# A hand-ordered attention and mixing kernel: order of work, PSUM banks and filling products laid anew

## Chip, core and metric

The kernel runs on one core of one Trainium2 chip. The metric is the device time of one execution in microseconds. The engines are TensorE (PE, matrix products; PEld is its weight load), VectorE (DVE), ScalarE (ACT), GpSimd (POOL) and SyncE (SP, here the one queue that issues all DMAs).

## What is computed

Eight batches of eight heads, 576 positions, head size 64. Attention with a mask over blocks of 64 positions comes first; its output, put together over the heads, goes through a mixing layer.

```
scores = scale * q @ k.T ; masked where block_i < block_j ; softmax over the last axis
x      = (attn @ v), heads side by side: (8, 576, 512)
theta  = x @ w_theta ; zr = x * cos(theta) ; zi = x * sin(theta)
y      = w_tok_r @ zr + w_tok_i @ zi        (over positions)
u      = x + y
out    = u + max(u @ w_ch, 0)
```

## The kernel before

**Tiling.** Two heads are one pair; there are 32 pairs (`p`), 64 heads (`n`), four pairs to a batch (`b`). The work is cut into 2757 named parts, each a few instructions, each with the parts that it needs, the PSUM banks that it takes and those that it leaves.

**A pair.** `q`, `k`, `v` load. `qh`, `ql`, `kh`, `kl` split q and k in two summands (from pair 12 on; before that the products are plain fp32). `sab`, `sc`, `sd` are the scores in three pieces (L596, L608): `sab` takes two banks for each head, `sc` one for each, `sd` one for both. `m` are negated row maxima (DVE, L634 or L626), `e` the exponentials (ACT, L638), which read the banks and leave them.

**A head.** `high` and `low` split the probabilities in two fp16 summands (`low` always on DVE, L665), `turn` transposes each by DMA (L669, SP queue). The first four pairs have `tp` and `cp` in their place: transposes on PE (L650) and copies out of PSUM (L657, L659). `weighted` are the products with V (L684), 42 or 45 small ones of 65 columns. All heads put them into bank 0, so head n+1 has to wait until `normalise` of head n has read it: add (L694 on DVE or L692 on ACT), reciprocal (L696), product (L701), and for odd heads a last piece (L704). `again` copies 64 rows (POOL, L710).

**V's scale.** For each batch `vz` sums |v| on ACT (L501), `vr` adds the two sums (DVE, L505), `vb` and `vm` spread the sum (L349, L355), `vc` makes a power of two of it (L362 to L371), and `vf` scales V (POOL, L576). Of the first batch all this stands ahead of head 0.

**A batch's mixing.** `theta` are the products for the angles (L784), five tiles, each in one bank; `turns` (ACT), `rest` (DVE, L800), `size` and `sines` (ACT, L818, L820) make cosine and sine; `z`, `zh`, `zl` (L830, L324 to L330, L843) multiply by x and split; `mix` are the products over positions (L853), in eight sums of five parts; `u` takes them (L866); `uh`, `ul` split; `c` are the channel products (L886), `out` adds (L892), `fin` scales, `store` writes. The mixing of a batch runs between the pairs of the next.

**The order is written out.** `order_of` sorts the parts by the numbers in `PLACES`, one for each part, and checks that each comes after what it needs. Every engine gets its own parts in this order and runs them strictly so; so does SP's queue. `BANKS` lists the PSUM bank for each taking part in that order. `RUNNING` lists filling products (L1107): `(11, 1, 3)` means that ahead of part 11 of the order three products of 512 columns go to bank 1, whose result nobody reads. Which engine does a part is told by `ON`, which the change doesn't touch.

Of the kernel before, what the change touches and what calls it, by code (L numbers as in the profile page):

```python
# [187 lines left out]


RUNNING = [  # L190
    (11, 1, 3), (15, 5, 4), (35, 0, 15), (43, 0, 1)
]
ON = {"w5": "DDADADADD",
      "wc": "DPDPPPDDP",
# [966 lines left out]
```

## Time and profile before

| | |
|---|---|
| median of the runs | 663.96 us (663.5, 663.96, 668.18) |
| the profiled execution | 662.92 us |
| its span, first to last instruction | 661.1 us |
| PE busy | 639.8 us, 7136 products |
| DVE, ACT, POOL busy | 568.9, 474.7, 319.9 us |
| filling products | 23 |

The profile is of one execution. An engine's busy time is the time in which at least one of its instructions ran; products on PE overlap, and their ends are modelled, so a short loss can hide in "busy". Idle time ahead of an instruction is shown with what ended it.

### The profile page before, as it was taken

To read this page: it belongs to the slowest core of one execution; us is meant where nothing else is said; L and a number is where in the kernel's file an instruction comes from. 1 tells how busy PE (TensorE), PEld (TensorE's weight loads), DVE (VectorE), ACT (ScalarE), POOL (GpSimd) and SP (SyncE) were. 2 spreads that over 40 slices of the span, in tenths; PEclk is the share of its full clock that TensorE was granted. 3 is DMA by queue.
4 is the path that set the end of the run, shared out by engine and by line. 5 is a ranking of instruction groups with operands and counts; after the bars stand their busy time and mean duration, and the time that the engine had idled before them with its cause. 6 is when DMAs were issued, how large, how long until landed. Compare 5 with 4: busy or idle time off the path is not lost.

```text
span 661.1 us, 17330 instructions
## 1 busy us (share of the span) xinstructions
PE 639.8 (97%) x7136; PEld 502.5 (76%) x7136; DVE 568.9 (86%) x891; ACT 474.7 (72%) x732; POOL 319.9 (48%) x341
## 2 busy tenths in 40 slices
PE   7999989999989999999999999999999999999997
PEld 4789757887678868787788768887778768785775
DVE  5899998999999999899988998999877989857624
ACT  4898797966998779666985679896976777525502
POOL 1422156642567437963455456447566354233900
PEclk9999989999999999999999999999999999999999
DMA  8874177999999998899946996999659986550002
GB/s 324 294 252 157 42 148 154 206 205 196 191 228 167 167 245 178 145 183 251 174 121 126 225 190 139 224 187 214 159 135 224 178 147 124 105 123 11 1 37 108
DMA packets 247647, 110.51 MB, mean 167 GB/s; under 512 B 229008, under 2 KB 229008, under 8 KB 247568
## 3 DMA queue, kind: packets, MB, share of 16 engines
q1 hardware_dynamic: 247568, 109.41, 75.7%
q8 instruction: 56, 0.92, 0.6%
q14 instruction: 23, 0.19, 0.1%
HBM read 43.06 MB, written 9.44 MB: 79 GB/s over the span
## 4 chain that ended last, share of the span: by engine, by line
PE 72%; DVE 12%; ACT 6%; DMA 5%; POOL 2%; issue 2%; SPq 0%; ACTq 0%; DVEq 0%; POOLq 0%
PE ps L853 28%; PE ps L784 12%; PE ps L886 11%; PE ps L684 11%; PE ps L596 9%; DVE m L634 4%; DMA w_raw<-in_w_tok 2%; DMA pt<-p 2%; DVE p L665 1%; ACT t L638 1%; DMA w_raw<-in_w_theta 1%; DVE wT_l L432 1%; PE ps L608 1%; ACT L638 1%; DMA q<-in_qT 1%
## 5 line engine op out<-in xcount | busy, mean ns | idle before, releaser
L638 ACT ACTIVATE t<-ps,m 128x320 f32<-128x320 f32 (+4 forms) x288 | 141.8, 554 | 46.7 <-DVE m L634 31.2
L853 PE MATMUL ps<-wT_h,zl 128*128 128x288 f16 x540 | 154.6, 286 | 1.5 <-POOL zl L843 1.5
L853 PE MATMUL ps<-wT_h,zh 128*128 128x288 f16 x540 | 154.9, 287 | 0.7 <-DVE sizes L362 0.7
L853 PE MATMUL ps<-wT_l,zh 128*128 128x288 f16 x540 | 154.5, 286 | 0.0
L634 DVE TENSOR_REDUCE m<-ps 128x2 f32<-128x640 f32 (+3 forms) x128 | 118.1, 945 | 16.3 <-PE ps L601 14.0
L853 PEld LDWEIGHTS <-zh 128*128 128x128 f16 x1080 | 105.9, 98 | 27.3 <-issue 0.9
L684 PE MATMUL ps<-v,pt 128*128 128x65 f16 (+2 forms) x2668 | 114.9, 202 | 7.3 <-DVE x_ring L701 2.2
L665 DVE SCALAR_TENSOR_TENSOR p<-t,p 128x1664 f16<-128x1664 f32 x56 | 110.1, 1967 | 0.4 <-ACT p L326 0.2
L886 PE MATMUL ps<-uhl,wch_h 128*128 128x288 f16 x512 | 95.3, 286 | 0.1
L684 PEld LDWEIGHTS <-pt 128*128 128x128 f16 x2436 | 82.3, 98 | 12.3 <-issue 6.3
L784 PE MATMUL ps<-wth_h,xt 128*128 128x512 f16 (+1 forms) x384 | 87.4, 345 | 0.0
L784 PEld LDWEIGHTS <-xt 128*128 128x128 f16 (+1 forms) x576 | 46.5, 102 | 43.3 <-issue 1.9
L326 ACT ACTIVATE p<-t 128x1664 f16<-128x1664 f32 x46 | 73.0, 1596 | 4.5 <-DMA pt<-p 3.8
L886 PE MATMUL ps<-uhl,wch_l 128*128 128x288 f16 x256 | 73.2, 286 | 0.0
L853 PEld LDWEIGHTS <-zl 128*128 128x128 f16 x540 | 52.9, 98 | 15.0 <-POOL zl L843 1.9
L886 PEld LDWEIGHTS <-wch_h 128*128 128x128 f16 x512 | 48.7, 98 | 13.3 <-issue 0.8
L784 PE MATMUL ps<-wth_l,xt 128*128 128x512 f16 (+1 forms) x192 | 57.3, 344 | 0.0
L710 POOL COPY x_ring<-x_ring 64x64 f32<-64x64 f32 x64 | 39.2, 613 | 36.7 <-DVE x_ring L701 21.2
L866 DVE SCALAR_TENSOR_TENSOR u<-ps,gain,u 128x288 f32<-128x288 f32 x64 | 31.5, 507 | 18.3 <-PE ps L853 18.0
L596 PE MATMUL ps<-kh,qh 64*128 64x288 f32 (+2 forms) x240 | 38.8, 312 | 2.9 <-ACT t L638 2.9
L596 PE MATMUL ps<-k,qh 64*128 64x224 f32 (+3 forms) x288 | 39.9, 407 | 1.5 <-DMA k<-in_kT 0.9
L794 ACT ACTIVATE aa<-ps,sizes 128x512 int32<-128x512 f32 (+1 forms) x40 | 25.2, 644 | 22.3 <-PE ps L784 22.1
(187 smaller groups left out, 1274.4 us busy)
## 6 DMA issues: line engine op xcount, KB each, us to landing
raw_v<-in_v SPq DMA_DIRECT2D x32, 384.0 KB, 4.5
q<-in_qT SPq DMA_DIRECT2D x32, 320.0 KB, 4.0
k<-in_kT SPq DMA_DIRECT2D x32, 320.0 KB, 3.9
out<-u SPq DMA_DIRECT2D x32, 288.0 KB, 3.9
w_raw<-in_w_tok SPq DMA_DIRECT2D x5, 576.0 KB, 5.4
p<-in_w_tok SPq DMA_DIRECT2D x4, 576.0 KB, 6.4
pt<-p SPq DMA_TRANSPOSE x112, 4.6
w_raw<-in_w_theta SPq DMA_DIRECT2D x2, 512.0 KB, 6.4
```

The source lines that it names most:

```text
L326: engine.mul(to, x, scale)
L596: nc.tensor.matmul(s[hh][:, col:col + n], lhsT=qq[rows, i * P:(i + 1) * P], rhs=kk[rows, k0:k0 + n], start=nn == 0 and (j == 0 or c == "ab ...
L634: nc.vector.tensor_reduce(out=m, in_=s, axis=AX.XY if i in (2, 3) else AX.X, op=ALU.max, negate=True)
L638: nc.scalar.activation(out=to, in_=s, func=AF.Exp, scale=1.0, bias=m)
L665: nc.vector.scalar_tensor_tensor(out=self.p[:, 1, :], in0=self.t, scalar=LIFT, in1=self.p[:, 0, :], op0=ALU.mult, op1=ALU.subtract)
L684: nc.tensor.matmul(to, lhsT=pp[:, block, :], rhs=x, start=nn == 0, stop=nn == n - 1)
L710: nc.gpsimd.tensor_copy(out=x[64 - 64 * hh:P - 64 * hh], in_=x[rows])
L784: nc.tensor.matmul(g[rows, 0:cols.stop - cols.start], lhsT=x[:, dt, part, i, rows], rhs=ww[:, dt, cols], start=(n == 0), stop=(n == 11))
L794: nc.scalar.mul(a[:, i, 0:n].bitcast(I32), bank("t", self.b, i)[:, 0:n], self.batch.turn)
L853: nc.tensor.matmul(g, lhsT=zz[:, kk, cols], rhs=ww[:, kk, ts], start=(n == 0 and kk == k0 and nn == 0), stop=(n == 4 and nn == 2))
L866: nc.vector.scalar_tensor_tensor(out=self.u(dt)[:, ts], in0=bank("y", self.b, dt, th)[:, 0:HS], scalar=g_y, in1=self.u(dt)[:, ts], op0=ALU ...
L886: nc.tensor.matmul(g[:, 0:HS], lhsT=ww[:, dt, e * P:(e + 1) * P], rhs=uu[:, dt, th * HS:(th + 1) * HS], start=(n == 0), stop=(n == 11))
```

## The change

Three lists are replaced: `PLACES` (2757 numbers), `BANKS` (361) and `RUNNING`. The functions, the parts, their needs, their engines and their instructions stay. The new order was laid starting from the executed one, with durations of its trace.

```diff
 PLACES = [
-    3, 2, 14, 22, 24, 61, 188, 190, 4, 5, 21, 30, 37, 65, 158, 178, 31, 28, 53, 60, 63, 106, 205, 259, 42, 45, 73,
...
+    3, 2, 16, 19, 21, 65, 162, 191, 4, 7, 25, 30, 32, 59, 155, 181, 29, 27, 54, 60, 62, 89, 200, 261, 42, 40, 70,
...
 ]
 BANKS = [
-    1, 3, 5, 6, 7, 3, 1, 5, 1, 7, 3, 5, 1, 2, 7, 3, 1, 7, 4, 5, 1, 3, 5, 5, 6, 4, 2, 6, 4, 1, 3, 4, 6, 1, 2, 3, 1,
...
+    2, 4, 6, 7, 1, 1, 5, 3, 5, 1, 3, 5, 7, 1, 2, 3, 4, 2, 4, 1, 3, 5, 7, 5, 6, 3, 1, 6, 4, 3, 1, 4, 6, 2, 3, 1, 4,
...
 ]
 RUNNING = [
-    (11, 1, 3), (15, 5, 4), (35, 0, 15), (43, 0, 1)
+    (8, 0, 3), (13, 0, 4), (18, 0, 5), (34, 0, 18), (38, 0, 1), (52, 0, 2), (56, 0, 2), (122, 1, 2), (369, 0, 5)
 ]
```

Sorted out into parts, the two lists give these orders at the places that the text below speaks of ("fill 4" are four filling products; the numbers behind a name are pair, head or batch, then pieces):

```
PE, start         old: fill 3, sab 0, fill 4, sd 0, sc 0, fill 15, tp 1 0, fill 1, tp 0 1, tp 0 0, tp 1 1, vm 0, sab 1
                  new: fill 3, sab 0, fill 4, sc 0, fill 5, sd 0, fill 18, tp 1 0, fill 1, tp 0 1, tp 0 0, fill 2, vm 0, tp 1 1, fill 2, sab 1
PE, head 9        old: theta 0 0, sab 5, sd 5, sc 5, weighted 8, weighted 9
                  new: theta 0 0, sd 5, fill 5, sab 5, sc 5, weighted 8, weighted 9
DVE, head 8       old: low 9, m 5 3, m 5 4, z 0 0 0, normalise 8 0, m 5 0, normalise 8 1, m 5 1, normalise 8 2
                  new: low 9, m 5 3, m 5 0, m 5 1, normalise 8 0, m 5 4, normalise 8 1, z 0 0 0, normalise 8 2
PE, head 10       old: sc 6, mix 0 0 1 3, mix 0 0 1 4, weighted 10, mix 0 1 1 0
                  new: sc 6, mix 0 1 1 0, mix 0 0 1 4, sd 6, mix 0 1 1 1, 0 1 1 2, 0 1 1 3, 0 1 1 4, weighted 10
ACT, head 19      old: high 21, sines 1 1, normalise 19 0      new: high 21, size 1 1, normalise 19 0, sines 1 1
DVE, head 19      old: low 21, normalise 19 1, 19 2, 19 3      new: low 21, normalise 19 1, 19 3, 19 2
PE, head 20       old and new: weighted 19, mix 1 1 0 0, weighted 20
POOL, zl 2 0 4    old: z 2 1 1, vb 4, again 13 0, zl 2 0 4     new: zl 2 0 0, fin 1 2, zl 2 0 4, again 13 1
PE, pair 19       old: sab 19, sd 19, c 2 3 0, c 2 0 0, weighted 36, sc 19
                  new: sab 19, c 2 3 0, weighted 36, c 2 0 1, c 2 0 0, sd 19, sc 19
PE, pair 27       old: weighted 51, c 4 3 0, sab 27, c 4 2 1, c 4 2 0, weighted 52, sc 27
                  new: sab 27, weighted 51, c 4 0 0, c 4 3 0, c 4 2 1, c 4 2 0, two of mix 5, sd 27, sc 27
PE, pair 31       old: sab 31, weighted 60, c 5 1 1, c 5 3 0, sd 31, sc 31
                  new: sab 31, c 5 3 0, c 5 1 0, c 5 1 1, weighted 60, c 5 0 0, sd 31, sc 31
SP, head 54       old: turn 54 0, v 31, turn 55 0, store 3 3, turn 54 1, turn 55 1
                  new: v 31, turn 54 0, turn 54 1, turn 55 1, turn 55 0
```

## Rows read from the trace of the kernel before

**Rows 1.** The page: span, and each engine's busy time.

```profile
span 661.1 us, 17330 instructions
...
PE 639.8 (97%) x7136; PEld 502.5 (76%) x7136; DVE 568.9 (86%) x891; ACT 474.7 (72%) x732; POOL 319.9 (48%) x341
```

**Rows 2.** Stretches: length, then PE, PEld, DVE, ACT, POOL busy (instructions), clock, DMA.

```profile
0.00:24.00 24.00, 19.57 (x110) 12.30 (x110) 14.68 (x21) 13.91 (x22) 6.10 (x25) 1.00 0.86 320
24.00:92.00 68.00, 66.82 (x552) 55.40 (x553) 64.67 (x113) 58.49 (x95) 19.41 (x41) 1.00 0.55 171
24.00:205.00 181.00, 173.98 (x1868) 139.37 (x1868) 171.01 (x271) 150.79 (x237) 82.85 (x100) 0.99 0.81 182
92.00:564.00 472.00, 460.38 (x5648) 363.60 (x5646) 432.43 (x668) 368.62 (x565) 261.54 (x246) 1.00 0.89 180
564.00:657.00 93.00, 93.00 (x836) 71.20 (x832) 56.30 (x89) 33.70 (x52) 32.84 (x31) 1.00 0.26 65
657.00:661.10 4.10, 0.07 (x1) 0.00 (x0) 0.83 (x2) 0.00 (x0) 0.00 (x0) 1.00 0.19 73
```

**Rows 3.** PE's waits: its line, releaser, us in total, times, longest.

```profile
PE ps L596 <- ACT t L638: 2.9, 3, 1.3
...
PE ps L684 <- DVE x_ring L701: 2.2, 1, 2.2
PE ps L684 <- DVE x_ring L704: 1.8, 1, 1.8
PE ps L684 <- DMA pt<-p: 1.8, 2, 1.2
PE ps L853 <- POOL zl L843: 1.5, 1, 1.5
PE ps L596 <- DMA k<-in_kT: 0.9, 1, 0.9
```

**Rows 4.** Order of time, PE, the start: start, duration, instruction, count, idle before.

```profile
8.49 1.81 PE L1107 MATMUL ps<-ones 128*128 128x512 bf16 x4
...
11.52 3.41 PE L1107 MATMUL ps<-ones 128*128 128x512 bf16 x15
...
15.07 1.09 PE L650 MATMUL ps<-ident_r,t 128*128 128x128 f32 x8
...
24.20 1.55 PE L684 MATMUL ps<-v,pt 128*128 128x65 f32 x12 [0.77 <-POOL v L576]
```

**Rows 5.** Order of time, DVE, the start.

```profile
18.70 0.15 DVE L505 TENSOR_REDUCE sizes<-sizes 128x1 f32<-128x2 f32 x1 [0.33 <-ACT unused L501]
```

**Rows 6.** Order of time, PE, scores of pair 5 and head 9's products.

```profile
88.28 2.00 PE L596 MATMUL ps<-k,qh 64*128 64x288 f32 x16
...
95.43 2.92 PE L684 MATMUL ps<-v,pt 128*128 128x65 f16 x45 [2.24 <-DVE x_ring L701]
```

**Rows 7.** The stretch behind head 9's wait, columns as in rows 2.

```profile
95.20:98.50 3.30, 3.07 (x47) 2.88 (x47) 3.30 (x6) 3.29 (x6) 0.82 (x2) 0.53 0.24 85
```

**Rows 8.** Order of time, DVE, last angle tiles and head 8's last step.

```profile
88.52 1.41 DVE L800 SCALAR_TENSOR_TENSOR rr<-ps,sizes,aa 128x512 f32<-128x512 f32 x2
...
94.97 0.41 DVE L701 TENSOR_TENSOR x_ring<-ps,r 128x256 f32<-128x256 f32 x1
```

**Rows 9.** Order of time, DVE, ahead of head 20.

```profile
183.54 1.88 DVE L665 SCALAR_TENSOR_TENSOR p<-t,p 128x1664 f16<-128x1664 f32 x1
185.49 0.19 DVE L696 RECIPROCAL r<-r 128x6 f32<-128x6 f32 x1
```

**Rows 10.** Order of time, DVE, a long low part.

```profile
478.22 2.87 DVE L665 SCALAR_TENSOR_TENSOR p<-t,p 128x1664 f16<-128x1664 f32 x1
```

**Rows 11.** Order of time, POOL and DVE, 125 to 131 us.

```profile
125.23 5.63 POOL L710 COPY x_ring<-x_ring 64x64 f32<-64x64 f32 x1 [0.15 <-DVE x_ring L704]
128.91 1.85 DVE L665 SCALAR_TENSOR_TENSOR p<-t,p 128x1664 f16<-128x1664 f32 x1
```

**Rows 12.** The page's groups: count, then busy us, mean ns, idle before.

```profile
L665 DVE SCALAR_TENSOR_TENSOR p<-t,p 128x1664 f16<-128x1664 f32 x56 | 110.1, 1967 | 0.4 <-ACT p L326 0.2
```

300 rows, old and new, of tables (BANKS, PLACES) are left out of this document.

## Prediction

> **What bounds the kernel now.** I read the page first, then the busy times by stretch, the waits of TensorE (PE) summed by cause, and the order of time where a wait is long. The page shows PE busy for 639.8 of 661.1 us [rows 1]. So PE's work is the floor, and a change that only orders the work can win no more than what PE loses: 21.3 us idle, and what its clock costs. The stretches show where [rows 2]. Between 564 and 657 us PE has no idle time at all. After 657 us come 4.1 us of last elementwise work and store, which no order removes. From 92 to 564 us PE is idle for 472.0 - 460.4 = 11.6 us, from 24 to 92 us for 1.2 us; the rest, 4.4 us, falls before 24 us. VectorE (DVE) is the next engine: from 24 to 205 us it is busy for 171.0 of 181 us, so it has 10 us to spare there, and PE can gain little from a repair that needs DVE sooner.
>
> The sums of PE's waits name the single losses [rows 3]: head 9 waits 2.2 us for head 8 to leave bank 0, head 20 waits 1.8 us for head 19, two heads wait 1.8 us together for their transposed probabilities (1.2 the longer), one mixing product waits 1.5 us for `zl` of batch 2, and the one-bank scores of pairs 19, 27 and 31 wait 2.9 us together for exponentials that must leave their banks. Behind head 9's wait the granted clock is 0.53 over 3.3 us [rows 7], mostly the lower level of 1.2 GHz; before that PE had stood idle for 2.24 us [rows 6]. At full clock the stretch would have been 3.3 x 0.47 = 1.55 us shorter.
>
> **The change, part by part.** No operation changes its engine, and the work of DVE, ScalarE (ACT), GpSimd (POOL) and the queue is the same. Exponentials and sines alternate 15 times in both orders, so I count no further table load. What is added is 19 filling products.
>
> *Start.* Up to the first transposes the old list has 3, 4 and 15 fillers, the new one 3, 4, 5 and 18. Fifteen took 3.41 us [rows 4], so one costs 0.22, and eight more 1.8 us. The transposes began at 15.07, 0.14 after the last filler ended, so PE would get to them about 1.7 us later. What is late next: DVE copies these transposes out, and behind the copies in its queue stands the sum of the sizes of V (L505, 18.70), which had 0.33 us of its own wait to give [rows 5]. From it run the spreading product, the power of two and the scaled V on POOL, for which head 0 waited at 24.20 [rows 4]. I take 1.7 - 0.14 - 0.33 = **+1.2** (0 if ScalarE's exponentials come that much later anyway, +1.7 if nothing gives). The other seven small fillers up to pair 2 stand in waits of this stretch, and PE idles 4.4 us there; without that cover they cost 7 x 0.22 = 1.5.
>
> *Pair 5 and heads 8 and 9.* In the new list the scores of pair 5 take a bank that DVE must first clear of an angle tile (`rest 0 0`, second of the two at 88.52 to 89.93) [rows 8]. PE began these scores at 88.28 in the old order [rows 6]; so now it waits about 1.4 us, and five new fillers (1.1 us) stand in that wait. The pair's scores thus end about 1.5 us later, its maxima too, and DVE does them ahead of head 8's normalisation. In the new order less stands between its three steps. It ended at 94.97 + 0.41 = 95.38 [rows 8]; I put it 0.75 later. PE then reaches head 9 about 0.45 us less early, waits 1.8 instead of 2.24 and, filled shortly before, should keep its clock: 0.75 - 1.55 = **-0.8**. If the clock falls all the same, +0.75; if DVE catches up, -1.5.
>
> *Waits that the new order takes away.* Head 10 goes six PE parts later, behind mixing products that were ready, so its 1.2 us are covered; head 54's other half is issued ahead of head 55's transposes, which covers the other 0.6. `zl 2 0 4` goes eight places forward on POOL and its product six parts later on PE: 1.5. Scores of pairs 27 and 31: the two-bank part moves forward past the weighted sum and two channel products (pair 27), and two more channel products come between the two parts (pair 31); pair 19 gets one channel product more in between. All 2.9 go. Sum **-6.2**. Without this cover each price returns singly.
>
> *A wait that stays.* For head 20 the new order puts head 19's first step ahead of the sines on ACT. But on DVE the low part (183.54, 1.88) still stands in front of head 19's reciprocal (185.49) [rows 9], and only one mixing product still covers it: **0** of the 1.8.
>
> *The other moves.* 430 of 617 PE parts change place (by 2.35 on average, nine in ten by at most six), 719 of 890 DVE instructions, 530 of 651 parts on ACT, 269 of 314 parts on POOL, 224 of 285 issues on SP's queue; 218 of 361 bank choices stay. Every one of them can make a wait that the old trace doesn't show. Loads and stores that move on SP (up to 18 places) I cost at nothing: they run beside a whole pair's work. If that cover is gone, one wait for `k` cost 0.9 [rows 3]. The other new waits have bounds: 0 from below; from above, as much as the moved places lost before, 6.2. I take **+2.3**, nearer the lower end, since most moves are a few places and the stretch from 564 us shows that PE can run 93 us without a wait [rows 2].
>
> Sum: 1.2 - 0.8 - 6.2 + 0 + 2.3 = -3.5 us. The profiled execution took 662.92 (its span 661.1 and 1.8 outside). So 659.4 for such an execution; the median of the runs shown, 663.96, lies 1.04 above it, which gives **660.4**.
>
> **Rivals.**
> *The repairs hold.* New waits cost nothing, and with the whole list made from real durations head 20's wait (1.8) and some 1.5 us of the many small waits go too: 1.2 - 0.8 - 6.2 - 3.3 = -9.1, median 654.9. For it: each of the larger waits has one clear cause, and most causes moved. Against it: DVE has only 10 us to spare up to 205 us, and an in-order queue rarely loses one wait without getting another.
>
> *Nothing comes of it.* As much comes back as goes: new waits 6.2, so 1.2 - 0.8 = +0.4, median 664.4. For it: the old order too has no filler behind pair 0 apart from the ones at the start, so these waits were not expected when it was laid; the new one has unexpected ones as well.
>
> *Slower: instructions of DVE and POOL grow where they newly meet.* Durations are not fixed here. The low part takes 1967 ns on average [rows 12], 1.85 at one place [rows 11], but 2.87 at 478.22 [rows 10]; a copy of 64x64 on POOL stood for 5.63 us from 125.23 and ended at 130.86, right after the low part on DVE that ended at 130.76 [rows 11]. A list laid with these durations holds only while the same instructions overlap. Place: heads 8 to 23, from 92 to 205 us, DVE's busiest part. Price: DVE's spare 10 us of 24 to 205 us are the point from which it decides; with all 16 low parts 1.0 us longer DVE would be 6 us over it. With the repairs of that stretch and later gone, +0.4 + 6 gives a median of 670.4 and more, some 671. Against it: on average the part is only 0.1 us above the short one.
> By the Trainium skill, page SBUF — State Buffer, section on the two separate sides, VectorE with two SBUF inputs and a GpSimd instruction lock a shared pair of ports for a whole instruction, and the other is fully blocked. By that rule every shift between the two queues can lengthen either; the trace agrees with its 5.63 us copy. Its outcome here is that rival, 671 against 660.4.
>
> **How the numbers follow.** Forecast (657.5 to 663): 0.47. Repairs hold (653.5 to 657.5): 0.25. Nothing comes of it (663 to 667): 0.21. Slower: 0.07. The range 653.5 to 667 takes in the first three, whose ends are new waits of 0 with the small ones gone, and new waits of 6.2 with head 9's clock not saved and some us more. It leaves out the last and the tails. About 1%, 6.6 us, is what a measurement of this kernel can tell from no change (three runs lie between 663.5 and 668.2). Faster than 657.3: 0.25. Slower than 670.6: 0.07. Within: 0.68.
>
> **What the profile of the changed kernel would show.** Start right: head 0's products about 1.2 us after 24.2. Pair 5 right: fillers around 89 to 91 us, then one wait of some 1.8 us, clock 1.00 all through. Repairs right: no wait of L684 for a transpose over 0.5 us, none of L853 for `zl`, L596's waits for L638 well under 2.9 us. Head 20: a wait near 1.8 us for L701 or L704. New waits: PE's idle time from 92 to 564 us at about 11.6 - 6.2 - 0.4 + 2.3 = 7.3. The forecast is wrong if that idle time is over 11 or under 4, or if DVE's busy sum (568.9) moves by more than 5 us.

## The result, and the profile after

The changed kernel takes 667.68 us (median of 20 runs, 666.75 to 669.33), the kernel before 663.29 beside it (20 runs, 661.36 to 668.18): a ratio of 1.0066 by the medians, 1.006 by the comparison, with a 95% interval of 1.0044 to 1.0075. It is slower by some 0.6%. I had forecast 660.4 with a range up to 667.0, so the time lies just above the range. The profiled execution has a span of 667.0 us against 661.1 [rows 1], 5.9 more. Of the first run's ten executions below, one took 815 us; its ratio leaves that one out, and its median without it is 663.97 in place of 664.25.

The page of the kernel after, span and busy times, and its group of the low part:

```profile
span 667.0 us, 17356 instructions
...
PE 643.3 (96%) x7155; PEld 504.0 (76%) x7155; DVE 577.3 (87%) x891; ACT 474.1 (71%) x732; POOL 329.9 (49%) x341
...
L665 DVE SCALAR_TENSOR_TENSOR p<-t,p 128x1664 f16<-128x1664 f32 x56 | 114.9, 2054 | 6.1 <-ACT p L326 5.9
```

PE's busy time grew by 3.5 us, with 19 more fillers in it, and its idle time by 2.4. But DVE's busy time grew by 8.4 us and POOL's by 10.0, with the same instructions on the same engines: they take longer than in [rows 1] and [rows 12]. The stretches answer to [rows 2], with one more that becomes the important one, 287 to 440 us, ahead of it the kernel before, behind it the kernel after:

```profile
287.00:440.00 153.00, 152.31 (x1850) 121.07 (x1848) 142.73 (x221) 117.90 (x181) 77.82 (x77) 1.00 0.88 181
```

```profile
0.00:24.00 24.00, 20.29 (x123) 12.94 (x124) 15.54 (x23) 14.99 (x23) 6.47 (x26) 1.00 0.87 325
24.00:92.00 68.00, 66.29 (x541) 54.80 (x543) 63.02 (x110) 57.37 (x95) 23.01 (x41) 1.00 0.57 176
92.00:564.00 472.00, 458.78 (x5590) 360.93 (x5587) 441.41 (x659) 362.93 (x559) 263.24 (x239) 1.00 0.88 177
287.00:440.00 153.00, 145.56 (x1738) 114.15 (x1736) 144.07 (x210) 110.09 (x169) 90.42 (x72) 1.00 0.81 172
```

From 92 to 564 us PE is idle for 13.2 us, where I forecast 7.3 and the old order had 11.6. From 287 to 440 us it is idle for 7.44 us, where the old order had 0.69: 6.75 more. Outside that stretch, from 92 to 564 us, idle time fell from 10.93 to 5.78 us; that is what the repairs were worth. POOL is busy 90.4 us there in place of 77.8, though PE gets less far.

PE's waits in the kernel after, which answer to [rows 3]:

```profile
PE ps L684 <- DVE x_ring L701: 7.0, 6, 2.7
...
PE ps L784 <- DVE rr L800: 1.9, 2, 1.1
PE ps L596 <- ACT t L638: 1.3, 1, 1.3
PE ps L886 <- DVE rr L800: 1.1, 1, 1.1
PE ps L784 <- DMA xt<-xp: 0.9, 1, 0.9
```

The waits for `zl` on POOL (1.5) and for transposed probabilities (1.8) are gone, and of the 2.9 us for exponentials none is left at its old place. In their stead heads wait for DVE's normalisation, two angle products and one channel product for a bank that DVE's `rest` (L800) must first leave, and one score for an exponential. Seven of these ten waits stand between 300 and 440 us; the three others are head 9's, head 20's and a small one.

To place the loss by stage I take, for every part on PE, the time to the next part's start less the median of its kind in the old trace, fillers with their full time (us lost, old list to new):

| stage, us | before | after | difference | my forecast |
|---|---|---|---|---|
| 0 to 40 | 13.75 | 13.11 | -0.6 | +1.2 |
| 40 to 120 | 5.81 | 4.69 | -1.1 | -2.0 (pair 5, heads 9 and 10) |
| 120 to 287 | 5.35 | 5.63 | +0.3 | -1.5 (`zl`) |
| 287 to 440 | 1.42 | 9.55 | +8.1 | -0.4 (pair 19) |
| 440 to 580 | 4.91 | 3.01 | -1.9 | -3.1 (pairs 27 and 31, head 54) |
| 580 to the end | 0.18 | 1.29 | +1.1 | 0 |
| new waits, no place given | | | | +2.3 |
| sum | 31.4 | 37.3 | +5.9 | -3.5 |

One stage makes the result. What happens in it, in order of time on DVE (first fence) and POOL (second fence) in the kernel after, at three of its waits:

```profile
297.95 2.10 DVE L330 TENSOR_SCALAR p<-t 128x1664 f16<-128x1664 f32 x1
...
306.97 1.89 DVE L665 SCALAR_TENSOR_TENSOR p<-t,p 128x1664 f16<-128x1664 f32 x1
308.77 0.22 DVE L626 TENSOR_REDUCE m<-ps 128x1 f32<-128x64 f32 x1
308.91 0.15 DVE L694 TENSOR_SCALAR r<-ps 128x6 f32<-128x6 f32 x1
308.98 2.79 DVE L561 SCALAR_TENSOR_TENSOR ql<-q,qh 128x640 fp32r<-128x640 f32 x1
...
383.44 5.86 DVE L665 SCALAR_TENSOR_TENSOR p<-t,p 128x1664 f16<-128x1664 f32 x2
```

```profile
297.68 1.48 POOL L770 TENSOR_TENSOR xp<-x_ring,xp 128x640 f16<-128x640 f32 x1 [3.10 <-ACT xp L324]
...
307.40 3.69 POOL L858 TENSOR_TENSOR u<-xt 128x1152 f32<-128x1152 f16 x1 [4.02 <-DMA out<-u]
...
384.61 2.94 POOL L858 TENSOR_TENSOR u<-xt 128x1152 f32<-128x1152 f16 x1 [3.81 <-DMA out<-u]
387.52 2.36 POOL L547 TENSOR_SCALAR qh<-q 128x640 fp32r<-128x640 f32 x1
```

The high part at 297.95 finds POOL at work until 297.68 + 1.48 = 299.16 and ends 0.9 us after that; alone it takes 1.01. POOL's sum at 307.40 (2.36 us where nothing disturbs it) finds DVE's low part at work until 308.86, and ends 2.23 after it, at 311.09; `ql`, which began at 308.98, ends 0.68 after that and took 2.79 in place of 0.81 us. The small instructions between them read PSUM and took their usual 0.22 and 0.15. The two low parts from 383.44 took 5.86 us in place of 3.76: the second had to let the sum end first (387.55), and POOL's `qh` behind it in turn ends only after the low part's end at 389.30 (2.36 us, where 0.73 is the shortest of its kind). Each looks like one engine that stands until the other's instruction ends.

By the Trainium skill, page SBUF — State Buffer, section on the two separate sides, VectorE and GpSimd share a pair of ports as an exclusive lock, which VectorE needs for an instruction in a 2-port performance mode or with two SBUF inputs (then only against a GpSimd instruction that reads SBUF), and whoever comes first keeps it for the whole instruction. These rows agree with it: `ql`, with two SBUF inputs, took 2.79 us in place of 0.81. The small instructions between, which read PSUM, kept their 0.22 and 0.15 us.

### The profile page after: what moved, and what is told of

Its sections match the earlier page's. It is cut to its first block, busy times and chain, and to the rows that moved or that the text cites. A ratio compares the mean times of both kernels' runs of the same rounds, so it can differ in the third digit from the quotient of the medians.

```text
span 667.0 us, 17356 instructions
## 1 busy us (share of the span) xinstructions
PE 643.3 (96%) x7155; PEld 504.0 (76%) x7155; DVE 577.3 (87%) x891; ACT 474.1 (71%) x732; POOL 329.9 (49%) x341
## 5 line engine op out<-in xcount | busy, mean ns | idle before, releaser
L684 PE MATMUL ps<-v,pt 128*128 128x65 f16 (+2 forms) x2668 | 114.4, 202 | 7.1 <-DVE x_ring L701 7.0
L665 DVE SCALAR_TENSOR_TENSOR p<-t,p 128x1664 f16<-128x1664 f32 x56 | 114.9, 2054 | 6.1 <-ACT p L326 5.9
L684 PEld LDWEIGHTS <-pt 128*128 128x128 f16 x2436 | 82.3, 98 | 12.7 <-issue 6.2
L710 POOL COPY x_ring<-x_ring 64x64 f32<-64x64 f32 x64 | 33.3, 521 | 51.8 <-DVE x_ring L704 31.2
L770 POOL TENSOR_TENSOR xp<-x_ring,xp 128x640 f16<-128x640 f32 x16 | 28.1, 1756 | 35.1 <-ACT xp L324 24.8
L830 POOL TENSOR_TENSOR rr<-rr,x_ring 128x512 f32<-128x512 f32 x18 | 27.9, 1554 | 29.7 <-ACT rr L820 26.1
```

Of the source, the lines that this page charges most:

```text
L665: nc.vector.scalar_tensor_tensor(out=self.p[:, 1, :], in0=self.t, scalar=LIFT, in1=self.p[:, 0, :], op0=ALU.mult, op1=ALU.subtract)
L684: nc.tensor.matmul(to, lhsT=pp[:, block, :], rhs=x, start=nn == 0, stop=nn == n - 1)
L710: nc.gpsimd.tensor_copy(out=x[64 - 64 * hh:P - 64 * hh], in_=x[rows])
L770: engine_of("xl", 5 * self.b + dt).tensor_tensor(out=low, in0=x, in1=high, op=ALU.subtract)
L830: engine_of("z", (2 * self.b + hf) * 5 + n).tensor_tensor(out=cd, in0=cd, in1=x, op=ALU.mult)
```

## The experiments

Theory A: the time is lost by the order of the stretch from 287 to 440 us, because DVE and POOL instructions that shut each other out meet there just ahead of PE's waits. Theory B: instructions are dealt anew wherever the list departs from its trace, in any order. A third view is that the places in the queues make the waits and the grown instructions only go with them.

| run | what it is | median us | ratio to before, 95% | PE idle, 287 to 440 us |
|---|---|---|---|---|
| before | | 663.3 | | 0.69 |
| after | | 667.7 | 1.0044 to 1.0075 | 7.44 |
| first | new list, 287 to 439 us from the old | 664.25 | 0.995 to 1.002 | 3.62, of it 2.8 at the seam |
| second | old list, that stretch from the new | 669.5 | 1.006 to 1.012 | 6.09 |
| third | new list, the old fillers | 667.5 | 1.004 to 1.010 | 6.82 |
| fourth | mixed list | 660.8 | 0.993 to 0.998 | 0.73 |
| fifth | four meeting POOL instructions cut | 663.7 | 0.997 to 1.002 | 3.93 |
| sixth | four other POOL instructions cut | 667.4 | 1.003 to 1.009 | 7.27 |
| seventh | mixed list with two repairs | 658.5 | 0.991 to 0.996 | 1.72 |
| eighth | first run, seam mended | 660.4 | 0.995 to 0.999 | 2.33 |
| ninth | new list, head 20 alone repaired | 667.3 | 1.002 to 1.008 | 7.10 |

In the profiles of the first four and the last three kernels all lines behind the lists stand six lower (L678 for L684); in the fifth and sixth they are a few lines off (L666 for L665, L560 for L561, L803 for L800).

**Which stretch.** A list is cut after so many parts; what follows is the other list's remaining parts in its own order and banks.

```diff
 first: the new list up to its 1,257th part (287 us)
-then the new list
+then the old list's order up to 1,900 parts (439 us), then the new list
```

> The new list, with the stretch from the 1,257th to the 1,900th part (about 287 to 439 us) in the old list's order and banks. Theory A, the loss is made by the order of that stretch: the new list's trace loses 9.4 us of TensorE's time between 300 and 440 us against 1.3 in the old one, so about 8 us come back: 659.6 us, and no wait over 0.6 us between 300 and 440 us. Theory B, instructions of VectorE and GpSimd are re-dealt wherever the list is not the one whose trace the durations came from, whichever order follows: the old stretch, met in a new phase, loses some 4 to 8 us as well: 664 to 668 us.

It took 664.25 us, which by itself is theory B's figure and not A's. But between 300 and 440 us no wait is longer than 0.4 us, as A had it; the time went right at the seam, where PE waited, and the clock fell for about 7 us behind it. Stretches (length, PE busy, clock, DMA), then PE's and DVE's waits from 284 to 290 us, of the first run:

```profile
288.00:292.00 4.00, 1.19 (x6) 0.78 0.50 116
292.00:296.00 4.00, 4.00 (x25) 0.50 0.75 180
296.00:300.00 4.00, 4.00 (x64) 0.87 0.12 23
```

```profile
PE ps L847 <- ACT t L632: 2.8, 1, 2.8
```

```profile
DVE kh L541 <- DMA k<-in_kT: 2.1, 1, 2.1
```

The old list issues the load of `k` for pair 18 at 276.8 us, ahead of the seam; in the joined list it came at 283.7, DVE's queue stood at `kh` with the maxima behind it, and the exponential and its bank came late. The eighth run moves that one load.

```diff
+load of k for pair 18 behind the turn of head 32's first part (42 places forward; 43 below)
```

> The first run (new list, 287 to 439 us from the old) with its seam mended: the load of k for pair 18, which at the seam came only at 283.7 us and held VectorE at kh 18 for 2.1 us, goes 43 places forward, behind the turn of head 32's first part. If the 2.8 us wait at 287 us and the lower clock behind it came of that load alone, the run falls from 664.25 by 2.8 and some 3 us of clock to about 659 us, as theory A had it for the stretch. If the old stretch doesn't fit behind the new list for other reasons, 662 us or more.

660.4 us: within 1.5 us of what theory A had for the stretch. PE still waits 1.2 us at the seam, and its clock stays. The stretch does fit behind the new list; one late load had cost over 3 us.

The reverse:

```diff
 second: the old list up to its 1,257th part
+then the new list's order up to 1,900 parts (432 us), then the old list
```

> The old list, with the stretch from the 1,257th to the 1,900th part (about 287 to 432 us) in the new list's order and banks. Theory A (that stretch's order loses the time): 663.3 + 8.1 = about 671 us, with waits of 0.7 to 1.5 us between 300 and 440 us as in the new list. Theory B (what matters is which instructions happen to meet, not the order of the stretch): anything between 663 and 671 us, with waits at other places than in the new list.

669.5 us, 6.6 above the old list that ran with it. The waits for `rest` and for the exponential are those of the new list to the digit, though everything ahead of them is the old order; heads wait 1.0 us in two waits, where the new list has 2.4 in three. PE's waits of the second run between 300 and 440 us:

```profile
PE ps L778 <- DVE rr L794: 1.9, 2, 1.1
PE ps L590 <- ACT t L632: 1.3, 1, 1.3
PE ps L880 <- DVE rr L794: 1.1, 1, 1.1
PE ps L678 <- DVE x_ring L695: 1.0, 2, 0.6
```

So which instructions meet is settled by the local order, nearly always (an exception stands in the last section). Theory B falls.

```diff
 fourth: the new list up to 502 parts (120 us)
+then the old order up to 1,900, then the new up to 2,595 (606 us), then the old
```

> The new list up to the 502nd part (about 120 us), the old one up to the 1,900th (432 us in its trace), the new one up to the 2,595th (606 us), the old one to the end. Losses by stretch in the two traces, new less old: -1.7 us up to 120 us, +0.3 from 120 to 300, +8.1 from 300 to 440, -1.9 from 440 to 580, +1.1 behind. Theory A (losses belong to the order of a stretch): 663.3 - 1.7 - 1.9 = about 659.7 us, faster than both. Theory B (durations are dealt anew at each seam): 663 us or more.

660.8 us, 2.1 below the old list beside it, faster than both lists, as theory A had it within 1.1 us. Places and banks were always exchanged together in these lists, so what the banks alone do is not tested.

**Whether the meeting makes the waits.**

```diff
 xs 3 0, xs 4 1 (L858):
-tensor_tensor(out=u, in0=high, in1=low, op=add)
+tensor_tensor(out=u[:, :, 0:72], in0=high[:, :, 0:72], in1=low[:, :, 0:72], op=add)
 z 3 1 1, z 4 1 0 (L830):
+cd, x = (a[:, 0:1, 0:1] for a in (cd, x))
```

> The new list whole, but four GpSimd instructions of 300 to 410 us do only a fraction of their columns (the two sums xs 3 0 and xs 4 1 an eighth, the two products z 3 1 1 and z 4 1 0 one column of one block), so part of the computation is left out. They are the ones that were running when VectorE's ql 19, ql 20, low 42 and z 4 0 0 took 2.0, 1.1, 2.1 and 1.1 us too long. Theory, the two engines shut each other out and these VectorE instructions make the waits: ql 19 goes from 2.79 to 0.81 us, low 42 from 3.97 to 1.88, and TensorE's waits of 0.82 (311 us), 0.74 (338), 1.20 (389) and 1.17 us (404) go: 667.7 - 3.9 = about 663.8 us. Rival, the waits come of the places in the queues alone: the times of VectorE may fall, but the waits stay and the time is 667 to 668 us.

663.7 us, forecast 663.8. DVE of the fifth run at the place of 306.97 to 308.98 above, and PE's waits from 300 to 436 us:

```profile
305.98 1.89 DVE L666 SCALAR_TENSOR_TENSOR p<-t,p 128x1664 f16<-128x1664 f32 x1
...
307.99 0.88 DVE L560 SCALAR_TENSOR_TENSOR ql<-q,qh 128x640 fp32r<-128x640 f32 x1
...
380.04 3.94 DVE L666 SCALAR_TENSOR_TENSOR p<-t,p 128x1664 f16<-128x1664 f32 x2
```

```profile
PE ps L685 <- DVE x_ring L702: 1.9, 2, 1.1
PE ps L597 <- ACT t L639: 1.3, 1, 1.3
```

`ql` is back at 0.88, the two low parts at 3.94, and all three waits for `rest` and one head's are gone. The two left heads' (1.9) and the exponential's (1.3) were not treated. The counterpart:

```diff
 the same cuts at xs 3 1, xs 4 0, z 4 0 2, and an eighth of the columns at xd 3 1
```

> The counterpart: the new list whole, with four other GpSimd instructions of the same stretch and the same kinds cut in the same way (the sums xs 3 1 and xs 4 0, the product z 4 0 2, and the scaling xd 3 1), so as much work is left out, 7.2 us of GpSimd's time, but beside none of them a VectorE instruction had grown. Theory, the two engines shut each other out: nothing changes at ql 19, ql 20, low 42 and z 4 0 0, the four waits stay, 667 to 668 us. Rival, GpSimd is simply late or its work in general disturbs: some 3 to 4 us less, as in the run beside it.

667.4 us. DVE's two low parts and PE's waits of the sixth run:

```profile
380.91 5.86 DVE L666 SCALAR_TENSOR_TENSOR p<-t,p 128x1664 f16<-128x1664 f32 x2
```

```profile
PE ps L787 <- DVE rr L803: 1.9, 2, 1.1
...
PE ps L894 <- DVE rr L803: 1.1, 1, 1.1
```

As much POOL work taken away, and nothing gained but one head's 0.7 us, which moved to another part of the same stretch (`ql 20` no longer met its product, since POOL came earlier). So it isn't POOL's load, nor the queue places or the banks alone, which are the same in both runs: the meetings make the waits, for 4.0 of the 8.1 us. The other half is argued and not shown: the rows show the same sign for head 33 (the high part above) and for the exponential of pair 21 (a low part of 3.14 us beside `kl` at 365.8), untested. Head 45's wait (1.0) is of another kind: DVE's normalisation stands behind a low part that itself waits 2.2 us for ACT.

**The cost by itself.**

```diff
+for vector, pool in ((low, None), (high, None), (evict, None), (None, add), (None, scale),
+                     (low, add), (high, add), (evict, add), (low, scale), (high, scale)):
+    gate()          # both engines wait for each other; ends with a 128x1 tensor_tensor on DVE
+    for _ in range(4): vector(); pool()
```

> Only the disputed cost, by itself; the kernel's own computation is left out. Three VectorE instructions (the low part of 128x1664 with two operands in SBUF; the high part with one, to f16; an eviction of 128x1024 from PSUM) and two GpSimd ones (the sum of 128x1152; the scaling of 128x640), four times each alone, and then in pairs. Theory, an engine that comes second stands until the other's instruction ends: low beside the sum takes 1.88 + 2.4 = 4.2 us each in turn, and the high part 1.0 + 2.4 = 3.4; the eviction and the sum beside it keep their own times. Rival, both engines share a rate: low and sum grow each by a part (low to 2.5 to 3 us), and the eviction grows too.

Order of time on DVE in that kernel (four low parts, high parts and evictions alone, then beside the sum), and the sum on POOL (alone, beside low, high and eviction):

```profile
9.19 7.67 DVE L33 SCALAR_TENSOR_TENSOR p<-t,p 128x1664 f16<-128x1664 f32 x4
...
17.66 4.21 DVE L36 TENSOR_SCALAR p<-t 128x1664 f16<-128x1664 f32 x4
...
22.66 5.00 DVE L39 TENSOR_SCALAR t<-ps 128x1024 f32<-128x1024 f32 x4
...
42.32 2.29 DVE L62 TENSOR_TENSOR t<-qr,xt 128x1 f32<-128x1 f32 x1 [0.46 <-POOL qr L61]
44.65 13.78 DVE L33 SCALAR_TENSOR_TENSOR p<-t,p 128x1664 f16<-128x1664 f32 x4
...
61.29 10.31 DVE L36 TENSOR_SCALAR p<-t 128x1664 f16<-128x1664 f32 x4
...
74.46 5.00 DVE L39 TENSOR_SCALAR t<-ps 128x1024 f32<-128x1024 f32 x4
```

```profile
28.17 9.65 POOL L42 TENSOR_TENSOR u<-xt 128x1152 f32<-128x1152 f16 x4
...
42.25 14.44 POOL L42 TENSOR_TENSOR u<-xt 128x1152 f32<-128x1152 f16 x4
...
58.89 11.84 POOL L42 TENSOR_TENSOR u<-xt 128x1152 f32<-128x1152 f16 x4
...
72.06 9.67 POOL L42 TENSOR_TENSOR u<-xt 128x1152 f32<-128x1152 f16 x4
```

Low parts and sums take 7.67 and 9.65 us alone; together they need from 42.25 to 58.43, 16.2 us, where strictly one after the other would give 17.3. The eviction and the sum beside it keep 5.00 and 9.67 us to the digit. The 4.2 us that I expected for each low part in turn was too much (3.45): the four stand for three sums only, since the gate's addition has taken the first, and 4 x 1.92 + 3 x 2.41 = 14.9 us came out as 13.78, some 0.16 less at each of seven changes of hands. The high parts give the same, 4 x 1.05 + 3 x 2.41 = 11.4 against 10.31. The plainest row is the 128x1 addition, 0.16 us alone: begun 0.07 us after a sum, it took 2.29. An instruction that comes second pays what is left of the other, however small it is itself. The high part has one input, and is held as well. The scaling on POOL gives the same: four low parts and four scalings, 7.67 and 3.14 us alone, take 9.28 and 7.68 beside each other.

**The fillers.**

```diff
 third: RUNNING of the new list
-3, 4, 5, 18, 1, 2, 2, 2 and 5 fillers at nine places
+3, 4, 15 and 1 at the old four
```

> The new list with the old list's filling products (3, 4, 15 and 1 in place of 3, 4, 5, 18, 1, 2, 2, 2 and 5). Theory A, the fillers pay: without them TensorE's clock rises about 2 us later at the start and falls to half behind head 9's wait, so head 0's products begin at 24.3 in place of 23.85 and 1.5 us are lost near 95 us: about 669 us, 1 to 2 us above the new list's 667.7. Rival, the fillers cost: the 19 extra products are 3.9 us of TensorE's time, of which some 2 come back: 665 to 666 us.

667.5 us: no difference from 667.7 by the median. The single executions hint that two effects cancel in it. At a mean clock of 0.999 or 1.000 the old fillers give spans of 663.8 to 664.1 us (three executions), the new ones 665.0 to 666.6; but where the clock fell more, at 0.992 to 0.995, the old ones give 666.7 to 669.5, and the new list's mean clock was never under 0.996. The third run's profile is one of those at 0.992. In it the clock fell at the start already:

```profile
20.00:24.00 4.00, 3.40 (x16) 2.92 (x18) 2.33 (x5) 4.00 (x7) 2.28 (x3) 0.57 0.71 285
```

Head 0's products began at 25.52 us there. So the 19 products seem to cost some 1.5 us and to give it back by keeping the clock up, a mixture of theory and rival that no run takes apart. In the profiled executions head 9's wait was 1.5 us with the new fillers and without, and the clock stayed at 1.00 behind it both times; so the five fillers ahead of pair 5 are not why the clock held there.

**Head 20, and a better list.**

```diff
 ninth (new list), DVE's order:
-low 21, normalise 19 (three steps)
+normalise 19 (three steps), low 21, and its transposing load behind it
```

> The new list with one change: VectorE's low part of head 21, which stood ahead of head 19's last steps at 181.84 us, goes behind them, and its transposing load with it. Theory: head 20's wait of 2.66 us falls by the low part's 1.8 to below 1 us, and the clock, which fell to half right behind that wait and cost 1.5 us, stays: 667.7 - 1.8 - 1.5 = 664.4 us. Rival: the clock falls at another wait instead, 665.9 us; or VectorE is only later elsewhere and gives all back, 667.7 us.

667.3 us: it gave nearly nothing. PE's wait of the ninth run from 180 to 190 us:

```profile
PE ps L678 <- DMA pt<-p: 2.4, 1, 2.4
```

In the new list it is `PE ps L684 <- DVE x_ring L701`, 2.7. DVE was done at 183.4 in place of 185.6 us, but head 20's own transposed probabilities, whose second load is issued from 179.0 to 181.0, had landed only when PE began at 185.0; in the new list's profile it landed at 185.5. Two causes lay behind one wait, and ended almost together. The clock did hold in this profile, and the span is 665.0 in place of 667.0, but neither is shown to be the edit's doing: behind the same wait of 2.7 us the clock held in the profiles of the sixth and the eighth run too, and the new list's own executions at a mean clock of 1.000 have spans of 665.0 to 666.3.

```diff
 seventh: the fourth run's list (to 2,552 parts, then old)
+normalise 19's first step ahead of the sines on ACT; low 21 behind normalise 19 on DVE, m 11 0 ahead of it
+zl 2 0 4 ahead of head 13's copy on POOL
```

> The mixed list of the run before (new to 120 us, old to 432, new to about 590, old to the end) with two waits of its own repaired. Head 20: head 19's first step goes ahead of the sines on ScalarE, and on VectorE the low part of head 21 goes behind head 19's last step; its 2.67 us should fall to about 0.5. Product of batch 2: zl 2 0 4 goes ahead of head 13's copy and two small parts on GpSimd, 1.65 us. If both hold and nothing comes in their place: 660.8 - 2.1 - 1.6 = 657.1 us. If the pushed instructions (low 21, zl 1 0 1) meet the other engine anew and give the gain back: 660 to 661 us.

658.5 us, 4.3 below the old list beside it and 1.4 above what I expected. Here head 20's loads are issued ahead of the next `q` and end up earlier: its wait is 1.0, again for the load. The product's 1.65 us are gone. All its `ql` take 0.79 to 0.83 us and the four sums on POOL of batches 3 and 4 take 2.36 to 2.62.

## Why the prediction was wrong

**What bounds it.** Right: PE's work is the floor, and the waits move. Wrong is the premise that the work of DVE and POOL is the same: with the same instructions they were busy 8.4 and 10.0 us longer.

**Start, +1.2: wrong in sign.** PE in the kernel after:

```profile
8.32 1.04 PE L1107 MATMUL ps<-ones 128*128 128x512 bf16 x4
...
23.85 0.88 PE L684 MATMUL ps<-v,pt 128*128 128x65 f32 x6
```

Head 0's products came at 23.85 in place of 24.20 us [rows 4], the sum at L505 at 18.57 in place of 18.70 [rows 5]. I priced the fillers at 0.22 us each without asking at which clock the products around them run: the new four took 1.04 us where the old four took 1.81 [rows 4], so PE already ran at the higher clock level, where one filler takes some 0.22 us. The first transposes were 0.48 late, not 1.7. The third run, with the old fillers, has the same median, so no gain at the start is shown by the time. Of the seven small fillers one stands in the old list too; six are added, 1.3 us and not 1.5.

**Pair 5 and head 9, -0.8: right in sum, partly for a wrong reason.** The wait is 1.5 (1.8 forecast, though scores 1.5 later and a normalisation 0.75 later make 2.24 + 0.75 - 1.5 = 1.5), head 9's products come at 96.04 (0.61 later; 0.75 forecast), and the clock is 1.00 from 95.2 to 98.5 us where it was 0.53 [rows 7]. That the fillers hold the clock there is not borne out: in the third run's profile it held without them.

**Repairs, -6.2: right.** All those waits are gone, and PE's idle time from 92 to 564 us without 287 to 440 fell by 5.2.

**Head 20, 0 of 1.8: wrong.** DVE in the kernel after:

```profile
181.84 2.86 DVE L665 SCALAR_TENSOR_TENSOR p<-t,p 128x1664 f16<-128x1664 f32 x1
```

The wait grew to 2.7, since the low part in front took 2.86 us in place of 1.88 [rows 9]. In the profiled execution the clock fell behind it instead of at head 9: 0.71 from 184 to 188 and 0.87 to 192 us. That is chance of the execution, as the sixth and eighth runs show. The low part was also not the only cause.

**New waits, +2.3 with bounds of 0 and 6.2: the step that failed.** They were 6.75 us of idle time, 8.1 us by the table, in one stretch alone, and what made them, for 4.0 us as the fifth and sixth runs show, are DVE and POOL instructions that stood for each other. The upper bound had no ground: that the moved places had lost 6.2 before says nothing of what they can lose. The lower half was argued from the stretch that begins at 564 us, where POOL and DVE have less to do (DVE 56 of 93 us [rows 2]).

**The rival that ended slower had the mechanism but not its place.** I put it at heads 8 to 23 and let it decide only if DVE's 10 us to spare were used up, with all 16 low parts 1 us longer, and gave it 0.07. DVE needs no such shortage: one `ql` or one low part that stands 2 us just ahead of a bank's release is a wait of 1 us, in any stretch where PE has less cover than that. My own sign was there: I had said that DVE's busy sum moving by over 5 us, or idle time over 11, would refute the forecast. They moved by 8.4 and to 13.2.

## What to carry to other kernels

When a list is laid from measured durations, take the durations of DVE and POOL apart into what an instruction costs alone and what it stood for the other engine; only the first survives a new order, and the second must be laid as a resource that one engine holds at a time, for instructions of the kinds that grew here, whose tensors all lie in SBUF. Look for it by the maximum beside the median of a line, not by its mean. Behind a wait that is to be repaired, look for the second releaser that ends almost at the same time, and when two lists are each good in different stretches, join them where their queues agree and look at the loads that cross the seam.

## What was not expected of the hardware

The sides of DVE's instructions differ cleanly in one trace. The kernel after, shortest, median and longest in ns of a line with SBUF operands (the first two) and of two that read PSUM:

```profile
L665 DVE SCALAR_TENSOR_TENSOR p<-t,p x56: 1846/1883/3967, 86.0 to 579.3; 128x1664 f16<-128x1664 f32 x56
L561 DVE SCALAR_TENSOR_TENSOR ql<-q,qh x20: 789/811/2792, 170.4 to 550.1; 128x640 fp32r<-128x640 f32 x20
L866 DVE SCALAR_TENSOR_TENSOR u<-ps,gain,u x64: 470/508/519, 110.2 to 651.4; 128x288 f32<-128x288 f32 x64
L892 DVE SCALAR_TENSOR_TENSOR u<-ps,u x64: 410/447/458, 146.9 to 663.0; 128x288 f32<-128x288 f32 x64
```

Most meetings also come back in other profiles with the same local order: the low part of head 42 took 3.96 or 3.97 us in the new list and in the second, third, sixth and ninth runs. Not all do: in the third run's profile `ql` of pair 19 took 0.81 us, not 2.79, though the order there is the new list's, and PE waited 1.3 us for an exponential near that place instead. And the engines don't take turns strictly: the 5.63 us copy on POOL [rows 11] stood through five longer DVE instructions on SBUF, with a reciprocal of 0.16 us between them, from the low part at 125.10 to the one that ended at 130.76, while in the kernel with the cost by itself low parts and sums alternate.

The clock moves the time of one and the same list: the old list's executions that ran beside the first run have spans of 659.1 to 660.4 us at a mean granted clock of 1.000 and of 663.8 to 666.7 at 0.986 or 0.987, as much as the change under study makes. So lists are best compared at the same clock: at 1.000 the new list's spans are 665.0 to 666.3 us, so its loss is not the clock's. Nor does the length of an idle time settle whether the clock falls: it fell behind 2.24 us at head 9 in the old list and behind 2.66 at head 20 in the new one, and held behind 2.42 to 2.67 at head 20 in the fourth, sixth, eighth and ninth runs.
